# RG-LRU with a top-1 mixture of experts on one core: fixed slots at known rows, squares of eight blocks summed on TensorE, six weight halves cut by VectorE, narrow slots spread

## The chip, the cores and the metric

One core of a Trainium2 chip runs the whole program. The metric is the device time of one execution in microseconds (us), the median of the runs shown.

## The reference, cut to what matters

```
# recurrence, x, r_gate, i_gate: (4, 5056, 256)
log_a = 8 * sigmoid(r_gate) * log(clip(sigmoid(a_param)))
a_t   = exp(log_a)
xg    = sqrt(max(1 - a_t*a_t, 1e-6)) * sigmoid(i_gate) * x
h     = a_t[:, t] * h + xg[:, t]                 # for each t: y[:, t] = h
# mixture, y as x: (20224, 256), 8 experts, w1: (8, 256, 1024), w2: (8, 1024, 256)
logits = x @ w_gate;  e = argmax(logits)
out[token] = softmax(logits)[e] * sigmoid(x @ w_output_gate)[e] * (relu(x @ w1[e]) @ w2[e])
```

All inputs and the output are float32.

## The kernel before

**Products.** An fp32 operand is multiplied by a power of two and cut into an upper and a lower f16 half; each product is then three f16 matmuls. The power of two comes from a bound on the operand's norm.

**Tokens.** The 158 tiles of 128 tokens form 20 chunks of 8 tiles, a chunk being two blocks of 512 tokens (128 partitions x 1024 numbers). For a block, SP loads three tensors; ACT does tanh twice (L569, L572), exp (L579), a square (L583) and a root (L588); DVE does two products (L575, L591) and the scan (L622). The bound on the block's norm follows: in the first eight chunks ACT squares the block once more and sums (`top`, L661), in the later ones DVE takes a maximum; one matmul spreads the sum (L294) and DVE makes the scale (L299, L300). ACT then writes the upper half (L675), DVE the lower one (L680), and PE transposes and takes the logits (L701); ACT copies the transposed rows out (L708).

**Routing.** Of each chunk, DVE picks the expert of every token, PE counts ranks (L742, L744), and DVE adds the rank to the running end of each expert's region in `xs`, a buffer in DRAM (`positions`, `counts`). POOL then writes the rows there by 8 indirect transfers (`scatter_rows`, L389), one a tile.

**Weights.** The 16 weight units (w1 and w2 of 8 experts) go through load, a sum of squares by PE (`gram`, L475, bf16 matmuls of 128x128 blocks with themselves), an ACT square of the 128x128 result (L481), a total (L484), the scale (L488), an upper half (L508) and a lower half on DVE (L522). `MODES` names the engine of the upper half for each unit: S is ACT, D is DVE. `BOUNDS` names for each chunk the engine of the norm.

**Expert work.** A slot is a run of rows of one expert: transposing load from `xs` (L1060), w1 from DRAM (L1075), first product (`ph`, L1103), relu on ACT (L1118) and its lower half on DVE (L1121), second product (`po`, L1147), scaling by ACT (`ot`, L1160), indirect store by POOL (L1163). `po` has one buffer of two 128x256 parts; the first `po` matmul of a slot waits until ACT has read both parts of the slot ahead. Most slots are planned on the chip: 63 of 256 rows, 25 of 128 and 4 of 64 ran. Before them come eight fixed slots of 128 rows, one an expert, for the first chunk (`turn`, L902 to L1023). `round_plan` (L879) works out their first rows and limits by nine DVE operations, SP reads each first row into a register (L913), and DVE clips the row numbers so that a row that isn't the slot's own goes nowhere (L980). Because a fixed slot may read past the rows that its expert has so far, the second chunk's scatters wait for all eight loads:

```
past = fetched.get(c - 1, []) + ([tiles["fill"]] if c < NC and "fill" in tiles else [])
```

**Order.** All work is given to a planner (`in_order`) with an engine, a cost, a rank and what it follows; it plays the program through and writes each engine's instructions in that order. The tables `UNIT_RANK`, `CHUNK_RANK`, `UNIT_LOAD`, `SLACK`, `LAG`, `PACE` and others are the ranks and delays. Engines run their instructions strictly in the written order.

## Time and profile before

| | |
|---|---|
| runs | 1047.46, 1047.15, 1046.22 us; median 1047.15 |
| profiled execution | 1047.38 us, of which the span is 1045.7 |
| PE, ACT, DVE, POOL busy | 92%, 69%, 66%, 36% of the span |
| granted TensorE clock, mean | 0.965 |

The span runs from the first to the last instruction of the profile; the execution's own time is 1.68 us longer. A share of busy time is a mean over stages that have different limits, so the stretches further down tell more than this table.

### The profile page before, as it was taken

To read this page: it belongs to the slowest core of one execution; us is meant where nothing else is said; L and a number is where in the kernel's file an instruction comes from. 1 tells how busy PE (TensorE), PEld (TensorE's weight loads), DVE (VectorE), ACT (ScalarE), POOL (GpSimd) and SP (SyncE) were. 2 spreads that over 40 slices of the span, in tenths; PEclk is the share of its full clock that TensorE was granted. 3 is DMA by queue.
4 is the path that set the end of the run, shared out by engine and by line. 5 is a ranking of instruction groups with operands and counts; after the bars stand their busy time and mean duration, and the time that the engine had idled before them with its cause. 6 is when DMAs were issued, how large, how long until landed. Compare 5 with 4: busy or idle time off the path is not lost.

```text
span 1045.7 us, 29645 instructions
## 1 busy us (share of the span) xinstructions
PE 966.7 (92%) x9892; PEld 869.4 (83%) x9892; DVE 694.9 (66%) x1714; ACT 720.6 (69%) x1153; POOL 372.9 (36%) x346
## 2 busy tenths in 40 slices
PE   2567668999999999999999999999999999999997
PEld 2467667888889899999899998999999988899886
DVE  6788886688678686776867768586785763322212
ACT  7989989998986868668677676677767542332222
POOL 0040153543445343443525334262443434311211
PEclk9658889999999999999999999999999999999999
DMA  9995469999788888788778687778798566647683
GB/s 326 376 337 128 111 201 280 277 321 263 245 267 228 247 258 214 258 225 256 233 230 261 198 272 221 241 249 227 245 218 246 162 174 198 168 145 246 240 221 132
DMA packets 196528, 244.25 MB, mean 234 GB/s; under 512 B 119182, under 2 KB 130447, under 8 KB 196384
## 3 DMA queue, kind: packets, MB, share of 16 engines
q1 hardware_dynamic: 180656, 199.13, 64.7%
q0 software_dynamic: 15728, 43.17, 12.5%
q8 instruction: 94, 1.54, 0.6%
q14 instruction: 50, 0.41, 0.1%
HBM read 79.09 MB, written 45.97 MB: 120 GB/s over the span
## 4 chain that ended last, share of the span: by engine, by line
PE 70%; DMA 10%; issue 7%; ACT 5%; SPq 3%; POOL 3%; DVE 3%; POOLq 0%; DVEq 0%; ACTq 0%
PE po L1147 33%; PE ph L1103 33%; PE pt L701 3%; DMA w1r<-in_moe_w_dram 2%; POOL xs L389 2%; DMA ws<-w1r 2%; DMA xs<-rows_all,posi 1%; DMA xt<-in_x_dram 1%; DMA w2r<-in_moe_w_dram 1%; DMA rt<-in_r_gate_dram 1%; SPq L1060 1%; POOL out_dram L1163 1%; ACT w1r L508 1%; ACT rows_all L708 1%; DVE h L1121 1%
## 5 line engine op out<-in xcount | busy, mean ns | idle before, releaser
L1103 PE MATMUL ph<-xt,ws 128*128 128x256 f16 (+2 forms) x4416 | 487.5, 256 | 8.3 <-DMA ws<-w1r 3.0
L1147 PE MATMUL po<-w2r,h 128*128 (+1 forms) x3720 | 492.7, 272 | 2.3 <-ACT ot L1160 1.1
L1103 PEld LDWEIGHTS <-ws 128*128 128x128 f16 x4416 | 377.2, 99 | 48.5 <-issue 8.9
L1147 PEld LDWEIGHTS <-h 128*128 128x128 f16 (+1 forms) x3720 | 358.0, 98 | 46.0 <-issue 3.5
L1121 DVE SCALAR_TENSOR_TENSOR h<-ph,h 128x512 f16<-128x512 f32 (+1 forms) x310 | 208.2, 679 | 190.0 <-ACT h L1118 189.4
L1163 POOL DMA_INDIRECT out_dram<-ot,mt x155 | 171.5, 1107 | 394.2 <-ACT ot L1160 335.3
L1118 ACT ACTIVATE h<-ph 128x512 f16<-128x512 f32 (+1 forms) x310 | 181.1, 588 | 107.6 <-PE ph L1103 107.2
L389 POOL DMA_INDIRECT xs<-rows_all,posi x158 | 180.1, 1140 | 200.1 <-ACT h L1118 91.4
L1160 ACT ACTIVATE ot<-po,osc 128x256 f32<-128x256 f32 (+1 forms) x155 | 68.3, 471 | 145.1 <-PE po L1147 125.0
L708 ACT ACTIVATE rows_all<-pt 128x512 f16<-128x512 f32 x158 | 92.5, 597 | 11.0 <-PE pt L701 7.1
L622 DVE TENSOR_TENSOR_SCAN it<-rt,last,it 128x512 f32<-128x512 f32 (+4 forms) x78 | 96.1, 1241 | 0.7
L701 PE MATMUL pt<-iw,xt 128*128 128x160 f16 x632 | 72.7, 242 | 11.7 <-ACT xt L675 5.8
L712 DVE TENSOR_REDUCE lz<-pt 128x16 f32<-128x64 f32 x158 | 34.3, 221 | 63.2 <-PE pt L701 39.1
L701 PEld LDWEIGHTS <-xt 128*128 128x128 f16 x632 | 54.3, 102 | 16.7 <-ACT xt L675 6.3
L579 ACT ACTIVATE rt<-rt,lam 128x512 f32<-128x512 f32 (+1 forms) x80 | 61.1, 802 | 0.2
L680 DVE SCALAR_TENSOR_TENSOR xt<-it,sc,xt 128x1024 f16<-128x1024 f32 (+1 forms) x40 | 50.7, 1267 | 11.9 <-ACT xt L675 11.6
L575 DVE SCALAR_TENSOR_TENSOR xt<-it,xt 128x1024 f32<-128x1024 f32 (+1 forms) x40 | 48.3, 1207 | 9.7 <-DMA xt<-in_x_dram 6.6
L591 DVE SCALAR_TENSOR_TENSOR it<-it,xt 128x1024 f32<-128x1024 f32 (+1 forms) x40 | 48.3, 1208 | 8.6 <-ACT it L588 8.6
L675 ACT ACTIVATE xt<-it,sc 128x1024 f16<-128x1024 f32 (+1 forms) x40 | 45.2, 1129 | 4.3 <-DVE sc L300 4.2
L583 ACT ACTIVATE it<-rt 128x1024 f32<-128x1024 f32 (+1 forms) x40 | 41.9, 1047 | 5.9 <-DVE xt L575 4.3
L569 ACT ACTIVATE rt<-rt 128x1024 f32<-128x1024 f32 (+1 forms) x40 | 42.0, 1049 | 5.5 <-DMA rt<-in_r_gate_dram 5.3
L588 ACT ACTIVATE it<-it,quarter 128x1024 f32<-128x1024 f32 (+1 forms) x40 | 44.5, 1133 | 0.3
(159 smaller groups left out, 712.8 us busy)
## 6 DMA issues: line engine op xcount, KB each, us to landing
ws<-w1r SPq DMA_DIRECT2D x184, 512.0 KB
rt<-in_r_gate_dram SPq DMA_DIRECT2D x39, 512.0 KB
it<-in_i_gate_dram SPq DMA_DIRECT2D x39, 512.0 KB
xt<-in_x_dram SPq DMA_DIRECT2D x39, 512.0 KB
w1r<-in_moe_w_dram SPq DMA_DIRECT2D x7, 1024.0 KB
w2r<-in_moe_w_dram SPq DMA_DIRECT2D x7, 1024.0 KB
xs<-rows_all,posi POOLq DMA_INDIRECT x158
out_dram<-ot,mt POOLq DMA_INDIRECT x155
```

The costliest lines, as they stand in the source:

```text
L389: op = nc.gpsimd.indirect_dma_start(out=xs[:, :], out_offset=bass.IndirectOffsetOnAxis(ap=pos, axis=0), in_=rows.bitcast(F32), in_offset=None,
L579: nc.scalar.activation(r[:, h], r[:, h], AF.Exp, scale=lam[:, h:h + 1], bias=lam[:, h:h + 1])
L622: nc.vector.tensor_tensor_scan(H[:, h, lo:hi], A[:, h, lo:hi], H[:, h, lo:hi], first, op0=ALU.mult, op1=ALU.add)
L680: nc.vector.scalar_tensor_tensor(halves()[:, 1], H(), s_of(), halves()[:, 0], op0=ALU.mult, op1=ALU.subtract)
L701: nc.tensor.matmul(pt[:, k, h * P:h * P + PIECE], lhsT=halves()[:, k, h, (j % 4) * P:(j % 4 + 1) * P], rhs=iw[:, h, :], start=h == 0, stop ...
L708: nc.scalar.activation(rows_all[:, row_at[j], 0:META].rearrange("p (k h d) -> p k h d", k=2, h=ND), src, AF.Copy)
L1103: nc.tensor.matmul(ph[:, i], lhsT=ws[:, f // 2 % 2, a, c, f % 2 * P:(f % 2 + 1) * P], rhs=xt[:, b * ND + c, 0:w], start=k == 0, stop=k == ...
L1118: newest["relu"] = nc.scalar.activation(part(0, f0), tiles["ph", s, f0], AF.Relu).ins
L1121: nc.vector.scalar_tensor_tensor(part(1, f0), tiles["ph", s, f0], 0.0, part(0, f0), op0=ALU.max, op1=ALU.subtract)
L1147: nc.tensor.matmul(po[0:pw, j], lhsT=hh[:, a, f % 4, j * P:j * P + pw], rhs=w2r[:, bass.ds(eo + (b * NF + f) * D, D)], start=f + j + a + b ...
L1160: nc.scalar.activation(ot[0:pw], tiles["po", s][0:pw, j], AF.Copy, scale=tiles["osc", s][0:pw, j, :])
L1163: op = nc.gpsimd.indirect_dma_start(out=out[:, :], out_offset=bass.IndirectOffsetOnAxis(ap=tiles["mt", s][0:pw, j, 1:2].bitcast(I32), axis=0),
```

## The change

- The first 128 rows of each expert in the first chunk go to an area of their own behind the regions, 128 rows an expert at an address that is known beforehand. `round_plan`, the register loads and the clip are gone; `positions` of the first chunk has three more DVE operations and `counts` one more. Only the first chunk's scatters wait (for the filling with zeros); the second chunk's wait for no load.
- `BOUNDS` names P for the first four chunks. PE then multiplies the upper bf16 halves of the block's eight 128x128 parts with themselves into one 128x128 sum (`energy`, after.py L678), ACT squares that and sums it (`spread`, L684).
- `MODES` gives the upper halves of six w2 units to DVE (one operation of 128x2048 each, L511).
- The narrow slots are put in at every fourth place among the last wide ones and no longer all at one place.
- New ranks, loads and delays everywhere.

```diff
-REGION = 21760
+REGION = 20736
-MODES = 'SSSSSSSSSSSSSSSS'
+MODES = 'SDSDSDSDSDSDSSSS'
-BOUNDS = 'AAAAAAAADDDDDDDDDDDD'
+BOUNDS = 'PPPPAAAADDDDDDDDDDDD'
-LAG = 0.00102
+LAG = 0.00107
-SLACK = (0.324, 1.234, 2.066, 1.637, 1.622, 0.589)
-PACE = 9.7e-05
+SLACK = (0.187, 0.464, 1.348, 1.897, 0.524, 0.04)
+PACE = 8.94e-05
-THIN_AT = 6
+THIN_AT = 12
+THIN_GAP = 3
...
-        past = fetched.get(c - 1, []) + ([tiles["fill"]] if c < NC and "fill" in tiles else [])
+        past = [tiles["fill"]] if c < ROUNDS else []
...
+            def energy(key=key, H=H, m=m):
+                norm_tile(key)
+                upper = H().bitcast(BF16).rearrange("p h (t two) -> p h t two", two=2)
+                k = 0
+                for h in range(ND):
+                    for f in range(0, m, P):
+                        blk = upper[:, h, f:f + P, 1]
+                        nc.tensor.matmul(tiles["norm", key][:, P:2 * P], lhsT=blk, rhs=blk, start=k == 0, stop=k == ND * m // P - 1, skip_group_check=True)
+                        k += 1
+
+            def spread(key=key):
+                am = tiles["am", key] = small.tile([P, 1], F32, name=f"am_{key[0]}_{key[1]}", tag="am", bufs=4)
+                pn = tiles["norm", key]
+                nc.scalar.activation(pn[:, 2 * P:3 * P], pn[:, P:2 * P], AF.Square, accum_out=am)
...
+            if c < ROUNDS:
+                nc.vector.scalar_tensor_tensor(beyond, carry, -float(P + c * E * P), fixed, op0=ALU.add, op1=ALU.subtract)
+                nc.vector.scalar_tensor_tensor(pos, rank_in, float(P), wide(beyond), op0=ALU.is_ge, op1=ALU.mult)
+                nc.vector.scalar_tensor_tensor(pos, pos, float(c * E * P), wide(fixed), op0=ALU.add, op1=ALU.add)
+                nc.vector.tensor_tensor(pos, pos, rank_in, op=ALU.add)
...
-                nc.sync.dma_start_transpose(xt[:, :, 0:P], xs[bass.ds(row, P), 0:META // 2].bitcast(F16)),
+                nc.sync.dma_start_transpose(xt[:, :, 0:P], xs[first:first + P, 0:META // 2].bitcast(F16)),
...
-            nc.vector.tensor_scalar(ids_, ids_, tiles["turn_lim", c][:, e:e + 1], float(N), op0=ALU.max, op1=ALU.min)
```

**ACT, around the last weight unit's square (L481 before, L482 after; `pg` is a unit's sum of squares, `w2r` an upper half of w2, `xt` a block's upper half, `am` a norm sum).** Before:

```order
69 L661 ACTIVATE xt_0_394,am_0_776<-it_0_322 128x1024
70 L481 ACTIVATE pg_754,sq_780<-pg_754 128x128
71 L508 ACTIVATE w2r<-w2r,wsc 128x2048
72 L675 ACTIVATE xt_0_394<-it_0_322,sc_806 128x1024
73 L481 ACTIVATE pg_782,sq_822<-pg_782 128x128
74 L569 ACT_TABLE_LOAD
75 L569 ACTIVATE rt_0_774<-rt_0_774 128x1024
76 L708 ACTIVATE rows_all<-pt_0_838 128x512
77 L708 ACTIVATE rows_all<-pt_1_844 128x512
78 L661 ACTIVATE xt_4_544,am_4_871<-it_4_459 128x1024
```

With the change:

```order
67 L482 ACTIVATE pg_732,sq_756<-pg_732 128x128
68 L684 ACTIVATE norm_0_764,am_0_792<-norm_0_764 128x128
69 L482 ACTIVATE pg_774,sq_799<-pg_774 128x128
70 L694 ACTIVATE xt_0_400<-it_0_328,sc_802 128x1024
71 L482 ACTIVATE pg_810,sq_829<-pg_810 128x128
72 L569 ACT_TABLE_LOAD
73 L569 ACTIVATE rt_0_753<-rt_0_753 128x1024
74 L732 ACTIVATE rows_all<-pt_0_838 128x512
75 L732 ACTIVATE rows_all<-pt_1_844 128x512
76 L579 ACTIVATE rt_0_753<-rt_0_753,lam 128x512 x2
```

The last weight square is row 73 before and row 71 now. Ahead of it stand three of the eight block squares and six `w2r` halves of 128x2048 before, and three small squares (L684) and no such half now, but eight table loads instead of six. Behind it stand five block squares and one such half before, five small squares and one half now.

**POOL, from the first chunk's scatters on (`xs` scatters, `out_dram` stores of the fixed slots).** Before:

```order
20 L389 DMA xs<-rows_all,posi_612 174080x264 x8
21 L1014 DMA out_dram<-ot_t_0_1082,mt_t_0_813 20224x256
22 L1014 DMA out_dram<-ot_t_1_1254,mt_t_1_831 20224x256
23 L1014 DMA out_dram<-ot_t_2_1462,mt_t_2_854 20224x256
24 L389 DMA xs<-rows_all,posi_1331 174080x264 x8
25 L1014 DMA out_dram<-ot_t_3_1588,mt_t_3_953 20224x256
```

With the change:

```order
20 L390 DMA xs<-rows_all,posi_658 168192x264 x8
21 L1018 DMA out_dram<-ot_t_0_1126,mt_t_0_852 20224x256
22 L390 DMA xs<-rows_all,posi_1194 168192x264 x4
23 L1018 DMA out_dram<-ot_t_1_1291,mt_t_1_868 20224x256
24 L390 DMA xs<-rows_all,posi_1194 168192x264 x3
25 L1018 DMA out_dram<-ot_t_2_1404,mt_t_2_885 20224x256
26 L390 DMA xs<-rows_all,posi_1194 168192x264
27 L1018 DMA out_dram<-ot_t_3_1566,mt_t_3_975 20224x256
```

The second chunk's eight scatters stood behind the stores of fixed slots 0, 1 and 2; now the last of them alone stands behind that of slot 2.

**PE, at the border of two wide slots in the middle of the program (`po` the second product, `ph` the first; one row for each group of six matmuls of a kind, or for their first).** Before:

```order
9973 L1147 MATMUL po_7727<-w2r,h_1_7644 128x256
...
10008 L1103 MATMUL ph_6_7864<-xt_33_7372,ws_1_7609 128x256
...
10020 L1103 MATMUL ph_0_7902<-xt_34_7674,ws_0_7714 128x256
...
10046 L1147 MATMUL po_7945<-w2r,h_0_7751 128x256
```

With the change:

```order
9294 L1151 MATMUL po_7221<-w2r,h_1_7172 128x256
...
9329 L1107 MATMUL ph_6_7323<-xt_30_6874,ws_1_7103 128x256
...
9341 L1107 MATMUL ph_0_7361<-xt_31_7038,ws_0_7218 128x256
...
9355 L1151 MATMUL po_7376<-w2r,h_0_7278 128x256
```

Between the last `po` of a slot and the first of the next stood 18 `ph` matmuls (6 of `ph_6`, 12 of `ph_0`); now 12 stand there (6 and 6). So it is at 33 of the borders of the 63 wide slots that run; at most others, transposes (L701, now L725) stand between as well, before and now, and six `ph` matmuls fewer.

## Rows read from the trace of the kernel before

**Rows 1.** Stretches of 25 and 100 us: busy us and instructions, PE clock, DMA share, GB/s

```profile
core 0: us, PE busy (x) PEld busy (x) DVE busy (x) ACT busy (x) POOL busy (x), PEclk, DMA share, GB/s
25.00:50.00 25.00, 12.83 (x122) 11.69 (x122) 18.07 (x30) 23.10 (x33) 0.00 (x0) 0.66 1.06 376
50.00:75.00 25.00, 16.42 (x143) 15.22 (x143) 22.27 (x61) 22.57 (x39) 12.76 (x8) 0.58 1.06 379
75.00:100.00 25.00, 17.57 (x192) 16.18 (x193) 21.45 (x42) 22.54 (x30) 1.47 (x1) 0.77 0.52 104
100.00:125.00 25.00, 17.91 (x214) 15.64 (x212) 23.07 (x56) 24.88 (x36) 2.21 (x2) 0.82 0.35 100
125.00:150.00 25.00, 18.21 (x205) 15.83 (x204) 19.30 (x54) 22.84 (x35) 12.72 (x12) 0.93 0.69 212
150.00:175.00 25.00, 19.31 (x220) 18.44 (x221) 17.81 (x37) 23.88 (x33) 12.52 (x11) 0.80 0.91 258
225.00:250.00 25.00, 25.00 (x272) 22.77 (x271) 18.67 (x41) 24.59 (x41) 11.42 (x10) 1.00 0.89 296
400.00:500.00 100.00, 100.00 (x972) 90.36 (x970) 71.53 (x179) 71.81 (x119) 38.47 (x34) 1.00 0.85 241
```

**Rows 2.** ACT's groups by form, 0 to 260 us: busy, mean ns, idle before

```profile
L508 ACT ACTIVATE w2r<-w2r,wsc 128x2048 f16<-128x2048 f32 x7 | 13.9, 1990 | 0.9 <-DVE w2r L522 0.9
L661 ACT ACTIVATE xt<-it 128x1024 f32<-128x1024 f32 x13 | 13.7, 1052 | 2.8 <-DVE it L622 2.8
L661 ACT ACTIVATION_READ_ACCUMULATOR xt<-it 128x1 f32 x13 | 2.5, 192 | 0.0
L481 ACT ACTIVATE pg<-pg 128x128 f32<-128x128 f32 x16 | 4.1, 258 | 4.9 <-PE pg L475 4.9
L481 ACT ACTIVATION_READ_ACCUMULATOR pg<-pg 128x1 f32 x16 | 3.0, 185 | 0.0
L588 ACT ACT_TABLE_LOAD x11 | 14.1, 1283 | 0.2
```

**Rows 3.** PE in order of time, the last weight unit's sum of squares

```profile
75.30 1.03 PE L475 MATMUL pg<-fw 128*128 128x128 bf16 x8 [0.67 <-DMA fw<-in_moe_w_dram]
```

**Rows 4.** ACT in order of time, up to the last weight unit's square

```profile
77.16 1.15 ACT L675 ACTIVATE xt<-it,sc 128x1024 f16<-128x1024 f32 x1 [0.53 <-DVE sc L300]
78.21 0.26 ACT L481 ACTIVATE pg<-pg 128x128 f32<-128x128 f32 x1
```

**Rows 5.** DVE's groups by form, 0 to 260 us

```profile
L522 DVE SCALAR_TENSOR_TENSOR w2r<-w2r,wsc 128x2048 f16<-128x2048 f32 x7 | 16.4, 2348 | 0.0
L522 DVE SCALAR_TENSOR_TENSOR w1r<-w1r,wsc 128x1024 f16<-128x1024 f32 x14 | 17.7, 1278 | 0.6 <-ACT w1r L508 0.6
L980 DVE TENSOR_SCALAR mt_t<-mt_t,turn_lim 128x1 int32<-128x1 int32 x8 | 1.6, 203 | 0.0
```

**Rows 6.** POOL in order of time: first scatter of the first two chunks

```profile
58.26 1.36 POOL L389 DMA_INDIRECT xs<-rows_all,posi  x1 [50.01 <-DVE carry L786]
...
128.85 1.07 POOL L389 DMA_INDIRECT xs<-rows_all,posi  x1 [2.53 <-DVE lz L712]
```

**Rows 7.** SP's queue: loads of fixed slots 0 and 7, load of planned slot 0

```profile
77.44 1.32 SPq L920 DMA_TRANSPOSE xt_t<-xs  x1
...
122.51 1.22 SPq L920 DMA_TRANSPOSE xt_t<-xs  x1
...
146.65 1.25 SPq L1060 DMA_TRANSPOSE xt<-xs  x1
```

**Rows 8.** PE in order of time at a border of two wide slots

```profile
500.42 2.13 PE L1103 MATMUL ph<-xt,ws 128*128 128x256 f16 x18
502.38 1.36 PE L1147 MATMUL po<-w2r,h 128*128 x11
```

**Rows 9.** ACT in order of time at the same border

```profile
500.67 0.84 ACT L1160 ACTIVATE ot<-po,osc 128x256 f32<-128x256 f32 x2 [1.92 <-issue]
501.40 0.60 ACT L1118 ACTIVATE h<-ph 128x512 f16<-128x512 f32 x1
501.88 1.07 ACT L583 ACTIVATE it<-rt 128x1024 f32<-128x1024 f32 x1
```

**Rows 10.** PE's waits from 250 to 1000 us: total, times, longest

```profile
PE po L1147 <- ACT ot L1160: 0.9, 1, 0.9
```

**Rows 11.** PE in order of time in the second narrow slot

```profile
994.41 0.35 PE L1103 MATMUL ph<-xt,ws 128*128 128x64 f16 x6 [0.39 <-DMA ws<-w1r]
```

More of the change, by code (lines that the diff above doesn't have):

```diff
@@ L31 @@
 RAW = 0
-TURNS = (840, 880, 920, 920, 940, 940, 940, 940)
+TURNS = (860,)
 RESERVE = {128:800,256:1500}
@@ L376, in tables @@
         nc.vector.tensor_scalar(carry, iota_e, float(REGION), None, op0=ALU.mult)
-        nc.vector.tensor_scalar(base, iota_e, float(REGION), None, op0=ALU.mult)
+        nc.vector.tensor_scalar(fixed, iota_e, float(P), float(E * REGION), op0=ALU.mult, op1=ALU.add)
         nc.vector.memset(zrow, 0.0)
@@ L397, in scatter_rows @@
                 ins, k.name, mybir.DependencyInfo(mybir.DependencyClass.Sync, mybir.DependencyReason.DATA),
-                reason="rows come over the filling, and behind the slots of fixed place that read past the rows of an expert",
+                reason="rows come over the filling",
             )
@@ L785, in counts @@
             pk = tiles["pk", c]
-            nc.vector.tensor_tensor(carry, carry, pk[:, nt * E:(nt + 1) * E], op=ALU.add)
+            held = pk[:, nt * E:(nt + 1) * E]
+            if c < ROUNDS:
+                nc.vector.tensor_scalar(beyond, held, -float(P), 0.0, op0=ALU.add, op1=ALU.max)
+                held = beyond
+            nc.vector.tensor_tensor(carry, carry, held, op=ALU.add)
         quick = rank + QUICK
@@ L796, in chunk @@
         wt = work("DVE", 0.85, weights, [zs] + copied, quick, uses=rused)
-        ps = work("DVE", 0.85, positions, [pk, chain["carry"]], quick, uses=[pu])
-        ct = work("DVE", 0.14, counts, [ps, chain["carry"]] + ([chain["plan"]] if chain["plan"] else []), quick, uses=[pu])
+        ps = work("DVE", 0.85 + (0.55 if c < ROUNDS else 0.0), positions, [pk, chain["carry"]], quick, uses=[pu])
+        ct = work("DVE", 0.14 + (0.15 if c < ROUNDS else 0.0), counts, [ps, chain["carry"]] + ([chain["plan"]] if chain["plan"] else []), quick, uses=[pu])
         chain["carry"] = ct
@@ L877, in plans @@
                 plan(group[k:k + GROUP])
[L879 to L900 removed]
     def turn(c, e):
         rank = ROUND_RANK[c] + e * TURN + 0.0001
[L905 removed]
+        first = E * REGION + (c * E + e) * P
         s = ("turn", c, e)
@@ L912, in fetch @@
         def fetch():
-            _, (row,) = nc.values_load_multi_w_load_instructions(
-                tiles["turn_row", c][0:1, e:e + 1], engines=(SP,), min_val=0, max_val=E * REGION - P,
-                skip_runtime_bounds_check_because="rows are counted on the chip",
-            )
             xt = tiles["xt16", s] = xtp.tile([P, 4, SLOT], F16, name=f"xt16_t{c}_{e}", tag="xt16")
@@ L925, in fetch @@
             after_scatters(loads, c)
-            fetched.setdefault(c, []).extend(op.ins for op in loads)
-        rows = [v for cc in range(c + 1) for v in routed[cc]]
-        fw = work("SP", 2.0, fetch, [ready, xold, mold] + rows, rank, dma=1.15, uses=[xu, mu, vuse])
-        fetches.setdefault(c, []).append(fw)
+        fw = work("SP", 1.3, fetch, [xold, mold] + routed[c], rank, dma=1.15, uses=[xu, mu])
         hus = [rings["hh"].new() for _ in range(2)]
@@ L1053, in fetch @@
             _, (row,) = nc.values_load_multi_w_load_instructions(
-                tiles["plan", s][0:1, 0:1], engines=(SP,), min_val=0, max_val=E * REGION - w,
+                tiles["plan", s][0:1, 0:1], engines=(SP,), min_val=0, max_val=last_row - w,
                 skip_runtime_bounds_check_because="rows are counted on the chip",
@@ L1223, in rglru_moe @@
     chunk(0)
-    if ROUNDS:
-        round_plan(0)
     scaled = []
@@ L1245, in rglru_moe @@
             chunk(c)
-            if c < ROUNDS:
-                round_plan(c)
         plans(c)
@@ L1254, in rglru_moe @@
         k = len(wide) - SPARE - THIN_AT
-        for s in wide[:k] + thin[:E - THIN_SPARE] + wide[k:] + thin[E - THIN_SPARE:] if thin else wide:
+        order = list(wide)
+        for i, s in enumerate(thin[:E - THIN_SPARE]):
+            order.insert(k + i * (THIN_GAP + 1), s)
+        for s in order + thin[E - THIN_SPARE:]:
             if s in spare and s < n_wide and not late:
```

105 lines of the change are left out of this document (47 added, 58 removed).

## Prediction

> **What bounds the kernel now.** I read the stretches first, because the page's means (PE 92%) mix stages with different limits. From 225 us on PE has no gap, and a stretch of the middle shows PE busy 100.00 of 100 us while ACT and DVE have a quarter free [rows 1]. There only fewer or cheaper matmuls would help, and the change removes none. So the time is PE's fixed work plus what PE loses ahead of 225 us, plus a tail. From 25 to 175 us PE is busy 12.8 to 19.3 of 25 us, at granted clocks of 0.58 to 0.93. ACT is busy 22.5 to 24.9 of 25 in the same stretches: it is the bound. DVE, at 21.5 and 23.1 of 25 between 75 and 125 us, is close behind. Up to 75 us the DMA engines are also full (shares 1.06 and 1.06).
>
> Second, ACT's groups by form give prices: 1.990 us for an upper half of w2, 1.052 + 0.192 = 1.244 for a block's square with its accumulator, 0.258 + 0.185 = 0.443 for a unit's 128x128 square, 1.283 for a table load [rows 2]. Third, PE's and ACT's rows in order of time show the last weight unit: its sum of squares waited 0.67 us for its load and ran from 75.30 to 76.33 [rows 3]; ACT took its square at 78.21, behind an upper half of a block that ended then [rows 4].
>
> **The sum, against the profiled execution of 1047.38 us (0.23 above the median, which I neglect).**
>
> *ACT.* Eight squares at 1.244 become eight like the units' 128x128 square at 0.443: 8 x 0.801 = 6.4 us less. Six halves less are 6 x 1.990 = 11.9. Two more table loads are 2.6 more. Together 15.7 us less on the engine that bounds. But ACT works in its written order, and the last weight's square is a meeting point. The order shows three squares, all six halves and both table loads ahead of it: 2.4 + 11.9 - 2.6 = 11.7 us. The load comes no sooner, as the DMA engines are full and the bytes of weights are the same, so I take this part to become a wait for DMA. What is kept of it is at most the 1.9 us from 76.33 to 78.21; I take 1.5. Behind it stand five squares: 5 x 0.801 = 4.0 us, at ACT busy 90% or more until PE is full, so all of it counts. **ACT: -5.5**, with 0 (another engine takes over) and -15.7 (the planner moved enough chunk work ahead that none of it waits) as ends.
>
> *PE.* Each of eight blocks gets eight 128x128 bf16 matmuls. A unit's eight take 1.03 us [rows 3], so 8.2 us in all, 5.2 of it behind the meeting point. There PE has 6 to 7 idle us in each 25 [rows 1], which hides them, unless one stands ahead of work that ACT waits for. Between 0 and +5.2 I take **+1.0**.
>
> *DVE.* It gets six 128x2048 `tensor_scalar` operations, which no row shows. The nearest row, its lower half of the same shape, takes 2.348, and a half as long one 1.278 [rows 5]; so 7.7 to 14.1 us more; I take 2.348, the same columns. By the order one stands just ahead of the last weight's scale and two behind it: 7.0. Eight clips at 0.203 [rows 5] and nine operations of `round_plan` of like size leave: 17 x 0.2 = 3.4 less; four operations in `positions` and `counts` add 0.8. Net +4.4 behind the meeting point, against 5.5 us idle between 75 and 125 us [rows 1]. It just fits; I take **+0.5**, with 0 and +4.4 as ends. Ahead of it 7.0 us more must fit into 25 to 75 us, where DVE had 9.7 idle.
>
> The Trainium skill, page "VectorE: DVE Perf Modes", section "The perf-mode tier table", gives an fp32 `tensor_scalar` of 2048 columns 1.227 us, half its two-tensor price. By that the six would be 7.4 us and this term 0; the sum would be 0.5 us lower. No row here shows it.
>
> *Fixed slots.* The first chunk's scatters began at 58.26 [rows 6], fixed slot 0 was loaded at 77.44 and slot 7 at 122.51 [rows 7]. The second chunk's scatters waited for that last load and began at 128.85 [rows 6]; planned slot 0 was loaded at 146.65 [rows 7]. Now only POOL's order holds them: the eighth stands behind the store of fixed slot 2. I expect planned slot 0's load some 10 us earlier. That is worth something only while PE has gaps and ACT has time for the relu, and ACT has none (23.9 of 25 from 150 us on). Between 0 and -5.7 (PE's idle of 150 to 175 us), I take **-1.0**, near the lower end because ACT decides.
>
> *Narrow slots.* They have one wait for weights in the rows, 0.39 us [rows 11]. Spread among wide ones they lose it: **-0.4**, between -0.8 and +0.5.
>
> *Borders of wide slots.* `po` has one buffer, so PE must be covered while ACT reads it. PE left the last `po` at 500.42, ACT had read both parts at 501.51, 1.09 us later [rows 9], and 18 `ph` matmuls covered 1.96 us, until 502.38 [rows 8]. In all of 250 to 1000 us this wait cost 0.9 us, once [rows 10]. Now 12 matmuls stand there, 1.96 x 12/18 = 1.31 us of cover: 0.22 us remain. If ACT is free at the border that is enough; I take **0**, with +13 (below) as the upper end.
>
> Sum: -5.5 + 1.0 + 0.5 - 1.0 - 0.4 = **-5.4, so 1042.0 us**.
>
> **The rivals.**
>
> *The covers are too short (slower).* At the border a block's square of 1.07 us comes a relu behind the reads [rows 9]; had it stood ahead of them, they would end up to 1.07 later and PE would stand 1.07 - 0.22 = 0.85 us. ACT is 72% busy in the middle [rows 1], about half of it in such long operations. If a quarter of the 62 borders are hit with 0.85, it costs 62/4 x 0.85 = 13 us: 1055. It outweighs the gain from 7.5/62 = 0.12 us a border on. For it: all borders lost six matmuls of cover, and a loss here is on the saturated engine, so nothing gives it back. Against it: at 29 of the 62 borders transposes still stand in between, and the order puts the second products there by a plan that knows ACT's work.
>
> *DVE or the first chunk takes over (no change).* DVE's net 4.4 us do not fit, since its operations also wait, and the first chunk's scatters start 4 us later, behind one more table load and more DVE work, with the fixed slots behind them. That eats all: about 1047.
>
> *The freed ACT time carries (larger gain).* If chunk work fills ACT's 11.7 us ahead of the last weight, about 7 of it would be kept besides: 1035. For it: the planner reordered everything. Against it: three block squares stand ahead of that point in both orders.
>
> *POOL is held up.* POOL writes the first chunk's scatters from 58.26 on [rows 6] while DVE's new operations run. If one kept POOL from its work as long as it lasts, two of 2.348 would make the fixed slots later by up to 4.7, of which about half is seen: 1042.0 + 2.3 = 1044.3. The Trainium skill, page "SBUF — State Buffer", section "Who interferes with whom", says that a DVE `tensor_scalar` in a two-port mode locks GpSimd out of shared ports for the whole instruction. No row of this kernel shows such a lock, and by the order most of the six don't stand beside the scatters.
>
> **How the numbers follow.** A measurement of this kernel can tell about 0.2%, 2.1 us, from no change. The forecast has 0.45 (its own range 1038 to 1046; 0.03 of it within 2.1 us of before), the larger gain 0.13, POOL held up 0.05, no change 0.19 (0.13 within, 0.06 slower), short covers 0.18. Faster: 0.42 + 0.13 + 0.05 = 0.60; same: 0.03 + 0.13 = 0.16; slower: 0.06 + 0.18 = 0.24. The range runs from 1033, under the larger gain, to 1054, which leaves out the worse half of the short covers.
>
> **What would show it.** Right: PE full from about 220 us on, ACT with gaps for DMA ahead of the last unit's square, at about 77; DVE over 22 of 25 between 75 and 125 us; the second chunk's scatters begun before 120. The covers show as a wait of `po` for ACT's `ot` from 250 us on, 0.9 us before: over 7 us would make me wrong. A last weight square well before 75 would mean the larger gain; scatters of the first chunk past 63 and PE full only at 225 the case of no change. A new price for the 128x2048 `tensor_scalar` corrects the DVE term.

## The result and the profile after

The changed kernel took 1052.13 us (median of 5, 1051.24 to 1055.96) where the kernel before took 1046.22 on the same chip: ratio 1.0051, 95% interval [1.0036, 1.0067]. It is slower by half a per cent; 1042.0 and a gain were forecast. On another chip the pair came out at 1.0036 [1.0021, 1.0052] (e12_again below).

Chips differ, for both kernels alike: before takes 1047 us on some (here called chips of the first kind) and 1061 to 1067 on others (the second kind), so every ratio below is taken on one chip.

The profile of the first result caught that run's slowest execution (1055.96, span 1054.3). I read the new kernel mostly from e12_again, the same kernel on a chip of the first kind, whose span of 1048.6 lies 2.9 over that of before (3.3 between the medians on its chip). Stretches of e12_again, columns as in [rows 1]:

```profile
core 0 of [0], span 1048.6 us
core 0: us, PE busy (x) PEld busy (x) DVE busy (x) ACT busy (x) POOL busy (x), PEclk, DMA share, GB/s
25.00:50.00 25.00, 14.27 (x131) 12.80 (x130) 20.79 (x36) 20.39 (x32) 0.00 (x0) 0.86 1.06 377
50.00:75.00 25.00, 18.26 (x155) 16.90 (x155) 21.95 (x60) 19.24 (x38) 8.26 (x8) 0.57 1.06 377
75.00:100.00 25.00, 18.15 (x199) 16.76 (x197) 24.11 (x36) 21.53 (x31) 0.99 (x1) 0.74 0.54 131
100.00:125.00 25.00, 14.08 (x151) 12.06 (x151) 22.10 (x55) 22.61 (x34) 8.48 (x8) 0.73 0.44 139
125.00:150.00 25.00, 20.07 (x267) 17.98 (x267) 22.70 (x59) 24.39 (x38) 7.72 (x7) 1.00 0.42 112
150.00:175.00 25.00, 19.94 (x243) 17.44 (x244) 18.95 (x34) 22.53 (x35) 10.67 (x10) 0.93 1.02 295
...
225.00:250.00 25.00, 21.26 (x205) 18.10 (x204) 17.72 (x37) 23.00 (x37) 11.14 (x11) 1.00 0.88 267
```

ACT did get its gaps: 20.39, 19.24 and 21.53 of 25 us up to 100, against 23.10, 22.57 and 22.54 [rows 1]. DVE rose to 24.11 between 75 and 100. The decisive row is the last: PE, which had no idle between 225 and 250 us before [rows 1], now loses 3.74 us there. And from 250 us to the end PE is busy for 786.76 us before and for 790.44 in e12_again: at 250 it has 3.7 us more work left. PE's waits of e12_again from 200 to 300 us (total, times, longest) say on what:

```profile
PE ph L1107 <- DMA xt<-xs: 2.4, 1, 2.4
PE ph L1107 <- DMA ws<-w1r: 2.1, 1, 2.1
PE po L1151 <- ACT h L1122: 1.0, 2, 0.7
```

The first wait is for the rows of a slot: the first slot that needs the fifth chunk's scatters. Its load in SP's queue, before and in e12_again, each in order of time:

```profile
242.44 1.30 SPq L1060 DMA_TRANSPOSE xt<-xs  x1
```

```profile
244.16 1.27 SPq L1064 DMA_TRANSPOSE xt<-xs  x1
```

In e12_again PE has nothing else to do when it gets there; before, other work lasted until it got there, and it shows no wait. PE in order of time, the first product of that slot, before and in e12_again:

```profile
245.86 3.44 PE L1103 MATMUL ph<-xt,ws 128*128 128x256 f16 x30
```

```profile
248.99 3.44 PE L1107 MATMUL ph<-xt,ws 128*128 128x256 f16 x30 [2.43 <-DMA xt<-xs]
```

I call the start of this load **the date**: the end moves with it. In every profile on chips of the first kind the rest of the span after it is nearly the same, 803 to 807 us, while the date moves by 14. (The last columns are worked out. A chunk's ranks are PE's `pk`: the second row `pk<-oh,before` in time for the second chunk, the fifth for the fifth.)

```
kernel (profile)                  pk, chunk 2   pk, chunk 5    date    date - pk 5    span   span - date
before                               106.09       217.44      242.44      25.0      1045.7      803.3
e9_before                            105.81       216.29      241.38      25.1      1044.7      803.3
e10 before, halves on DVE            108.62       219.71      244.84      25.1      1048.9      804.1
e12 changed                          105.91       216.24      244.16      27.9      1048.6      804.4
e13 changed, 18 matmuls at borders   106.86       219.29      249.18      29.9      1053.8      804.6
e11 changed, slots' steps moved      111.17       218.47      246.41      27.9      1052.6      806.2
changed, first result                106.20       219.24      248.32      29.1      1054.3      806.0
e15 changed, halves on ACT           111.63       222.98      251.93      29.0      1058.0      806.1
e14 changed, both parts undone       114.26       226.12      255.09      29.0      1062.1      807.0
```

One trace is not a median: e12, e13 and the first result have the same order up to the slots ahead of the date, and their dates still lie 5 us apart (the last two are the slowest executions of their runs). So a date tells little below some 5 us, and the 3.7 us by which the last column varies are as large as the loss. The size of the loss comes from the medians; the traces tell where it arises.

So the first question is why freeing ACT did not make the chunks earlier. **ACT's gain arrives at the second chunk's logits and is lost in DVE's order right there.** Up to that chunk's `pk`, ACT's groups by form add up to 102.0 us before and 91.9 in e12_again: 10.1 less. Without the table loads it would be 91.8 against 76.5, 15.3 less, but the new order has 12 loads of 1.283 us up to there where the old one has 8. And `pk` comes at 105.91 against 106.09, no earlier. DVE in order of time, before (L723 is the last step that needs ACT's part, L736 what `pk` waits for):

```profile
102.45 0.22 DVE L723 TENSOR_SCALAR un<-sc,gun 128x8 int32<-128x8 int32 x1
102.58 2.58 DVE L522 SCALAR_TENSOR_TENSOR w1r<-w1r,wsc 128x1024 f16<-128x1024 f32 x2
105.08 0.22 DVE L732 SCALAR_TENSOR_TENSOR eq<-df,rev 128x64 f32<-128x64 f32 x1
105.34 0.22 DVE L735 TENSOR_REDUCE mx<-eq 128x8 f32<-128x64 f32 x1
105.59 0.22 DVE L736 TENSOR_TENSOR oh<-eq,mx 128x64 f16<-128x64 f32 x1
```

and in e12_again (the same two steps are L747 and L760):

```profile
97.44 0.23 DVE L747 TENSOR_SCALAR un<-sc,gun 128x8 int32<-128x8 int32 x1
97.58 1.22 DVE L591 SCALAR_TENSOR_TENSOR it<-it,xt 128x1024 f32<-128x1024 f32 x1
98.83 2.46 DVE L622 TENSOR_TENSOR_SCAN it<-rt,last,it 128x512 f32<-128x512 f32 x2
101.32 0.17 DVE L625 COPY last<-it 128x2 f32<-128x2 f32 x1
101.41 1.22 DVE L575 SCALAR_TENSOR_TENSOR xt<-it,xt 128x1024 f32<-128x1024 f32 x1
102.56 0.27 DVE L984 TENSOR_SCALAR osc_t<-mt_t,undo 128x1 f32<-128x1 f32 x1
102.74 2.47 DVE L523 SCALAR_TENSOR_TENSOR w2r<-fw,wsc,w2r 128x1024 f16<-128x1024 f32 x2
105.13 0.22 DVE L756 SCALAR_TENSOR_TENSOR eq<-df,rev 128x64 f32<-128x64 f32 x1
...
105.63 0.22 DVE L760 TENSOR_TENSOR oh<-eq,mx 128x64 f16<-128x64 f32 x1
```

`un` is 5.0 us earlier, about the 5.5 that were forecast for ACT. But between `un` and `oh` lie 8.19 us now and 3.14 before: the third chunk's gates and the last cut of a w2 unit have been put there. PE sees nothing of the gain; it stands for that `oh` (PE in order of time, e12_again):

```profile
96.94 1.50 PE L951 MATMUL ph_t<-xt_t,w1r 128*128 128x128 f16 x24
105.91 0.23 PE L766 MATMUL pk<-oh,before 128*128 128x64 f16 x1 [7.47 <-DVE oh L760]
106.27 1.01 PE L678 MATMUL norm<-it 128*128 128x128 bf16 x8
111.01 0.59 PE L295 MATMUL norm<-am,ones 128*128 128x1 f32 x2 [3.73 <-ACT norm L684]
```

So at this chunk nothing is gained. (The `pk` of this one chunk does not decide the end alone: see e11 below.) **What is lost on top lies further on, between the fifth chunk's ranks and the date:** 25.0 to 25.1 us in the three traces in the old order, 27.9 to 29.9 in the six in the new one. Before, PE's ranks of that chunk and then the first and the last of its eight scatters on POOL:

```profile
217.44 0.19 PE L742 MATMUL pk<-oh,before 128*128 128x64 f16 x1
```

```profile
220.91 0.97 POOL L389 DMA_INDIRECT xs<-rows_all,posi  x1 [0.30 <-issue]
...
236.41 1.15 POOL L389 DMA_INDIRECT xs<-rows_all,posi  x1 [0.30 <-issue]
```

and in e12_again:

```profile
216.24 0.19 PE L766 MATMUL pk<-oh,before 128*128 128x64 f16 x1
```

```profile
221.13 0.96 POOL L390 DMA_INDIRECT xs<-rows_all,posi  x1 [2.32 <-issue]
...
238.28 1.91 POOL L390 DMA_INDIRECT xs<-rows_all,posi  x1 [0.30 <-issue]
```

In e12_again the ranks are 1.2 us earlier than before and the date is 1.7 later. Of these 2.9 us, 1.4 lie between the ranks and the first scatter and 1.7 between the first and the last, among which POOL has three stores of slots instead of two. This is read from the traces; no run here moves these steps by themselves.

The new operations themselves are short. DVE's and ACT's groups by form from 0 to 260 us and PE's groups of the whole span, e12_again:

```profile
L511 DVE TENSOR_SCALAR w2r<-w2r,wsc 128x2048 f16<-128x2048 f32 x6 | 7.7, 1282 | 0.1
```

```profile
L684 ACT ACTIVATE norm<-norm 128x128 f32<-128x128 f32 x8 | 2.1, 264 | 2.2 <-PE norm L678 2.0
L684 ACT ACTIVATION_READ_ACCUMULATOR norm<-norm 128x1 f32 x8 | 1.5, 193 | 0.0
```

```profile
L678 PE MATMUL norm<-it 128*128 128x128 bf16 x64 | 7.1, 276 | 0.0
```

### The profile page after: what moved, and what is told of

Its sections match the earlier page's. It is cut to its first block, busy times and chain, and to the rows that moved or that the text cites. A ratio compares the mean times of both kernels' runs of the same rounds, so it can differ in the third digit from the quotient of the medians.

```text
span 1054.3 us, 29719 instructions
## 1 busy us (share of the span) xinstructions
PE 973.7 (92%) x9956; PEld 873.4 (83%) x9956; DVE 698.0 (66%) x1707; ACT 711.2 (67%) x1149; POOL 366.1 (35%) x346
## 4 chain that ended last, share of the span: by engine, by line
PE 73%; DMA 9%; ACT 8%; issue 4%; DVE 3%; SPq 1%; POOL 1%; POOLq 0%; ACTq 0%; DVEq 0%
PE po L1151 34%; PE ph L1107 33%; PE pt L725 3%; DMA ws<-w1r 2%; DMA xt<-in_x_dram 2%; DMA w1r<-in_moe_w_dram 2%; ACT rows_all L732 1%; DMA w2r<-in_moe_w_dram 1%; ACT rt L579 1%; PE ph_t L951 1%; PE po_t L1001 1%; POOL out_dram L1167 1%; DVE xt L575 1%; DVE xt L699 1%; ACT it L588 1%
## 5 line engine op out<-in xcount | busy, mean ns | idle before, releaser
L1151 PE MATMUL po<-w2r,h 128*128 (+1 forms) x3720 | 505.1, 272 | 5.3 <-ACT h L1122 1.6
L1107 PE MATMUL ph<-xt,ws 128*128 128x256 f16 (+2 forms) x4416 | 499.1, 255 | 10.5 <-DMA ws<-w1r 8.5
L1167 POOL DMA_INDIRECT out_dram<-ot,mt x155 | 166.6, 1075 | 343.4 <-ACT ot L1164 279.5
L725 PE MATMUL pt<-iw,xt 128*128 128x160 f16 x632 | 71.5, 240 | 10.3 <-DVE xt L699 3.4
L736 DVE TENSOR_REDUCE lz<-pt 128x16 f32<-128x64 f32 x158 | 34.0, 222 | 55.5 <-ACT rows_all L732 26.6
L725 PEld LDWEIGHTS <-xt 128*128 128x128 f16 x632 | 53.2, 101 | 16.1 <-issue 6.0
L572 ACT ACTIVATE it<-it 128x1024 f32<-128x1024 f32 (+1 forms) x40 | 42.2, 1055 | 3.7 <-DMA it<-in_i_gate_dram 3.6
```

Source lines behind the costliest of these rows:

```text
L725: nc.tensor.matmul(pt[:, k, h * P:h * P + PIECE], lhsT=halves()[:, k, h, (j % 4) * P:(j % 4 + 1) * P], rhs=iw[:, h, :], start=h == 0, stop ...
L1107: nc.tensor.matmul(ph[:, i], lhsT=ws[:, f // 2 % 2, a, c, f % 2 * P:(f % 2 + 1) * P], rhs=xt[:, b * ND + c, 0:w], start=k == 0, stop=k == ...
L1151: nc.tensor.matmul(po[0:pw, j], lhsT=hh[:, a, f % 4, j * P:j * P + pw], rhs=w2r[:, bass.ds(eo + (b * NF + f) * D, D)], start=f + j + a + b ...
L1167: op = nc.gpsimd.indirect_dma_start(out=out[:, :], out_offset=bass.IndirectOffsetOnAxis(ap=tiles["mt", s][0:pw, j, 1:2].bitcast(I32), axis=0),
```

## The experiments

Theories at the start: (O) the new order costs, the parts save; (W) one piece of it, the late last w1 halves, holds the slots' weights; (B) the shorter covers at the borders cost; (A) ACT's time ahead of the last weight's square is worth nothing. (The letters in the quoted expectations are those of each text by itself.) Ranks set the whole order, so most kernels below leave the order alone and change one thing in place.

**1. On a chip of the second kind (before 1061.27).** e1_again is the changed kernel unchanged.

> The changed kernel once more, as the yardstick of this batch. Every theory: the median within 1050 to 1054 us. The profile taken before was of an execution of 1055.96 us, 4 us over the median; if the 23 us by which the first weights of planned slots were loaded later (158.04 us against 135.10) are a property of the order and not of that one execution, they stand here again at 155 to 161 us, and PE again waits 6 us or more for slot weights ahead of 260 us.

Measured 1074.11, 1.0112 [1.0081, 1.0144]: the loss is more than twice as large on this kind of chip. The expected times were for the other kind. The named signs did not come either: the first weights are loaded at 167.17, and PE waits 2.5 us for slot weights ahead of 260 us. (On a chip of the first kind they are loaded at 157.42, in e12_again.)

e2_w1_early gives three w1 units an earlier rank:

```diff
-UNIT_RANK = (..., 2125.187, ..., 2071.655, 94.077, 1911.079, 778.463)
+UNIT_RANK = (..., 700.0, ..., 700.0, 94.077, 700.0, 778.463)
```

> The changed kernel with the ranks of the last three w1 units alone set from 2125, 2072 and 1911 to 700, so that their halves are cut earlier and the slots' first weight loads, which need all w1 halves, stand ahead of the slots' row loads in SP's order. Theory A (late w1 halves keep the planned slots off PE until 163 us): the first slot weights are loaded at 130 to 145 us, the first product of planned slot 0 begins by 153, and the time falls by 4 to 8 us, to 1044 to 1048. Theory B (the new norm by PE holds up PE's queue, or the missing cover of the wide slots costs): the time stays within 2 us of 1052.

e3_old_ranks has the changed structure with all ranks, loads and delays of before, e4_new_ranks the reverse.

```diff
-UNIT_RANK = (-32.393, -264.014, -294.491, 2128.445, ...)
+UNIT_RANK = (-418.188, 1238.039, 483.025, 96.75, ...)
```

> The changed kernel's structure (own rows of the fixed slots, norm by PE for eight blocks, six upper halves by DVE, narrow slots spread) with all ranks, loads, slacks and paces of the kernel before. Theory A (the new ranks cost, the structure saves): 1038 to 1045 us. Theory B (the structure costs): 1050 us or more.

> The kernel before with the new ranks, loads, slacks and paces and nothing else. Theory A (the new ranks cost 5 to 15 us by themselves): 1052 to 1062 us. Theory B (the structure costs and the ranks are good): at or under 1046 us.

Measured: e2 1101.32, 1.0369 [1.0334, 1.0405]; e3 1077.39, 1.0144 [1.0105, 1.0182]; e4 1098.09, 1.0345 [1.0307, 1.0382]. Each lets the planner write the whole order anew. None comes near a gain: e2 and e4 are slower than the changed kernel (1.0112), e3 is not told apart from it (intervals overlap). So both readings of e2 failed, and e3 and e4 tell only that orders written from other ranks lie 1.4 to 3.7% over before; they do not separate (O) from (W). From here on I moved works by hand.

**2. On another chip of the second kind (before 1060.72),** with e5_again as yardstick.

> The changed kernel once more as the yardstick of its batch: 0.3 to 1.4% over the kernel before.

Measured 1073.35, 1.0117 [1.0095, 1.0139].

e6_w1_moved moves only the late w1 cuts forward, and three weight loads of slots ahead of the first planned rows in SP's queue:

```diff
+    early = [at[v] for v in (("hi", 12, 1), ("lo", 12, 1), ("hi", 14, 0), ("lo", 14, 0), ("hi", 14, 1), ("lo", 14, 1))]
+    loads = [at["ws", 0, 0], at["ws", 0, 1], at["ws", 1, 0]]
...
+    k = order.index(at["lo", 12, 0]) + 1
+    order[k:k] = early
+    k = max(order.index(at["xs", 0]), k + len(early))
+    order[k:k] = loads
```

> The changed kernel in the very same order but for nine works: the last three w1 halves (ACT and DVE) stand directly behind the first half of the unit ahead, and the three first weight loads of planned slots stand directly ahead of the first row load of a planned slot in SP's queue; nothing else moves. Theory A (the late w1 halves keep planned slots off PE): first slot weights at 130 to 140 us, first planned product 5 to 10 us sooner, 3 to 8 us less than the changed kernel in the same batch. Theory B (ACT and DVE have no time for them earlier, what they push back costs as much): within 2 us of it.

Measured 1080.07, 1.0190 [1.0173, 1.0207]: 6.7 us worse than e5, where a gain or no change was expected. (W) falls: the late weights (157.42 in e12_again, 135.10 before) are not what costs, and cutting them earlier takes time from the chunks. In e6 the third chunk's `pk` comes at 158.92, in e5 at 150.42.

e7_cover puts 18 matmuls between the `po` of two blocks again, in PE's order alone:

```diff
+    for w in [w for w in order if w.tag and w.tag[0] == "po" and w.tag[2] == 0 and w.tag[3] == 256]:
...
+        if v.tag[0] == "ph":
+            order.insert(n + 1, w)
+            order.pop(k)
```

> The changed kernel in the same order, but at each border of two 256-row slots the first group of second products is put behind the next group of first products, so that 18 matmuls stand between the last second product of a slot and the first of the next, as before the change. Theory C (the cover of 12 is too short where ACT is called late): 3 us or more less than the changed kernel on a chip where the border shows a gap of 0.3 us or more, and nothing (within 2 us) on a chip where it shows none. Theory A: within 2 us on either.

Measured 1068.82, 1.0083 [1.0066, 1.0100]: 4.5 us better than e5; the intervals overlap slightly. So on this chip the longer cover probably pays, but not in the way (B) says. A border in e5, PE and then ACT in order of time:

```profile
518.61 1.47 PE L1107 MATMUL ph<-xt,ws 128*128 128x256 f16 x12
520.25 0.92 PE L1151 MATMUL po<-w2r,h 128*128 x6 [0.17 <-ACT ot L1164]
```

```profile
519.36 0.84 ACT L1164 ACTIVATE ot<-po,osc 128x256 f32<-128x256 f32 x2 [2.51 <-PE po L1151]
```

The 12 matmuls do not quite cover ACT's two reads, but by 0.17 us only, under the 0.3 that the expectation named. From 260 us on all waits of `po` for ACT's `ot` are 0.8 us in e5 and 0.6 in e7, so the 4.5 are not there. Where they come from is open.

e8_undone keeps the changed order and undoes both parts in place: ACT scales the six halves and squares the four chunks' blocks, the 64 matmuls are gone.

```diff
-                by_scale(hi_by, d[:, 0], fw)
+                by_scale("ACT", d[:, 0], fw)
...
-                nc.scalar.activation(pn[:, 2 * P:3 * P], pn[:, P:2 * P], AF.Square, accum_out=am)
+                nc.scalar.activation(tiles["xt", key][:, :, 0:m], H(), AF.Square, accum_out=am)
```

> The changed kernel in the same order, with the two parts that take work off ACT undone in place: ACT itself cuts the six w2 halves and squares the four chunks' blocks over 128x1024, each at the place in the order where the new operation stood; the 64 matmuls are gone. ACT does 15.8 us more ahead of 175 us. Theory A (ACT's freed time only became waits): within 3 us of the changed kernel. Theory D (ACT is still the bound and the freed time counts): 5 us or more over the changed kernel.

Measured 1080.28, 1.0192 [1.0176, 1.0208]: 6.9 us worse than e5, as theory D has it. The parts do save, in this order.

**3. On a chip of the first kind (before 1047.74).** e9_before is the kernel before, for its profile.

> The kernel before itself, for a profile from the chips on which it takes 1061 us and not 1047. Every theory: within 0.5% of the kernel before. If the 14 us more come from the same places as the changed kernel's, PE loses some of them ahead of 250 us and some at the transposes that wait for DVE's lower halves from 300 to 860 us, and none at the borders of the wide slots, where 18 matmuls stand.

Measured 1047.5, 1.0003 [0.9991, 1.0015]. The chip was of the first kind, so the question about the slower chips got no answer: no profile of the kernel before from the second kind exists here.

e10_before_modes takes the order of before and gives the six halves to DVE in place:

```diff
-                by_scale(hi_by, d[:, 0], fw)
+                by_scale("DVE" if u in (1, 3, 5, 7, 9, 11) else hi_by, d[:, 0], fw)
```

> The kernel before in its own order, with one part of the change put in place: DVE cuts the upper halves of the same six w2 units (six operations of 1.28 us in place of six of 1.99 us on ACT). Theory D (ACT is the bound and freed time counts): 3 to 8 us less than before. Theory A (freed time ahead of the last weight's square only becomes a wait, as forecast): within 2 us of before.

Measured 1049.6, 1.0016 [1.0005, 1.0027]. 11.9 us taken from ACT gain nothing in the old order; it is even 1.9 slower, and `pk` of the second chunk comes 2.5 later than in before (108.62). That fits (A) as to the time, but the trace shows ACT waiting for DVE and not for the weights' load. ACT in order of time, e10, ahead of the last weight's square, which came at 78.21 before [rows 4] and now comes at 82.31:

```profile
81.26 1.15 ACT L675 ACTIVATE xt<-it,sc 128x1024 f16<-128x1024 f32 x1 [5.12 <-DVE wsc L488]
82.31 0.26 ACT L481 ACTIVATE pg<-pg 128x128 f32<-128x128 f32 x1
```

e11_turn1 moves fixed slots' steps in the changed kernel, so that PE has work in the hole at 98 us:

```diff
+    group = [at[v] for v in (("ht", 1, 0), ("hl", 1, 0), ("ht", 1, 4), ("hl", 1, 4), ("ht", 2, 0), ("hl", 2, 0))]
+    group += [at["pt", 1, f] for f in range(8)]
...
+    k = order.index(at["pk", 1])
+    order[k:k] = group[6:]
...
+    order[k:k] = group[:6]
```

> The changed kernel in the same order but for 14 works around 98 us: ACT's three relus of fixed slots 1 and 2 and DVE's lower halves of them stand ahead of the last w2 unit's cut, and PE's second products of fixed slot 1 stand ahead of the ranks of the second chunk, for which PE waited 7.5 us with the clock falling behind. Theory E (the new order of the first 130 us leaves PE idle where work was there, and that is lost for good): 4 to 9 us less than the changed kernel (ratio to before of 1.003 to 1.008 where the changed kernel has 1.0115). Theory A (ACT's total up to 250 us decides, PE's idle here is made up): within 2 us of it.

Measured 1054.76, 1.0068 [1.0051, 1.0085], against 1.0051 [1.0036, 1.0067] and 1.0036 [1.0021, 1.0052] of the changed kernel on such chips: no gain, so theory E fails. PE's wait for `oh` shrank from 7.5 to 4.1 us, a new one of 2.9 for ACT came ahead of it, and `pk` of the second chunk came 5 us later (111.17). The date is still inside what the changed kernel shows by itself (246.41; 244.16 and 248.32), so a late `pk` of this one chunk is made up again here.

**4. Parts and order apart, on a chip of the first kind (before 1047.25).** All four on one chip.

> The changed kernel once more, the yardstick of this group. 1.005 of before if the chip is one of the faster kind (before near 1047), 1.011 if before is near 1061.

> Eighteen matmuls again between the po of a block and the next, nothing else moved. If the borders cost something only where ACT starts its read of the last po late (the slower chips), this is the changed kernel within 1 us on a chip with before near 1047, and 4 to 5 us under it on a chip with before near 1061. If the cover pays everywhere, 4 to 5 us under it on either.

> The new order with the old parts: ACT scales the six halves and squares the four chunks' blocks, the 64 matmuls are gone. If the order is the loss and the parts give back, this is 6 to 8 us over the changed kernel and 11 to 13 over before (1.011 of before on a fast chip). If the parts are worth nothing, it is the changed kernel within 2 us.

e15_halves_undone is e8's first edit alone.

> Of the two parts only the halves are undone, in place: ACT scales all six again (6 x 1.99 = 11.9 us more on ACT, 6 x 1.28 = 7.7 us less on DVE). If only what lies behind the last weight's square counts (the reading of the prediction), the halves are worth little and this is 0 to 2 us over the changed kernel, while the squares carry the 6 to 8 of the fully undone one. If any ACT time of the first 175 us counts, the halves carry two thirds: 4 to 5 us over.

Measured:

```
before                                          1047.25
e12_again          1.0036 [1.0021, 1.0052]      1050.54
e13_cover          1.0051 [1.0033, 1.0069]      1053.54
e15_halves_undone  1.0090 [1.0071, 1.0110]      1057.20
e14_all_undone     1.0133 [1.0110, 1.0156]      1062.32
```

This settles (O). With the old halves and squares the new order is 15.1 us slower than before (the new rows of the fixed slots and the spread narrow slots are in it too); the two parts give back 11.8 of it, the halves 6.7 (1057.20 less 1050.54), the squares 5.1. The direction was expected, the sizes were not: 6 to 8 for both and at most 5 for the halves. On the chip of e8 the same two parts gave back 6.9. And (B) costs nothing here: with the long cover the kernel is no better (3.0 us over e12, where 1 was expected; intervals overlap), and PE's waits of e12_again from 260 us on hold only this row for it (total, times, longest):

```profile
PE po L1151 <- ACT ot L1164: 0.6, 2, 0.4
```

The trace of e14 shows the order's cost at the same place of DVE as above:

```profile
105.79 0.23 DVE L738 TENSOR_SCALAR un<-sc,gun 128x8 int32<-128x8 int32 x1
...
113.98 0.22 DVE L751 TENSOR_TENSOR oh<-eq,mx 128x64 f16<-128x64 f32 x1
```

`oh` is at 105.59 before, 113.98 here and 105.63 in e12_again. Of the order's 8.4 us, 3.3 lie ahead of `un` and 5.0 between `un` and `oh`; the parts bring `un` forward by 8.35 (105.79 to 97.44), which just makes up for it. Further on in e14 against before, 8.7 us stand at the fifth chunk's ranks, 12.7 at the date and 16.4 at the end of the span.

**5. Can the swallowed time be had back?** On a chip of the second kind (before 1065.62). e16_chunk1_first takes the second chunk's small steps out of the way:

```diff
+    names = ("cn", "pk", "ps", "ct", "sm", "zs", "wt")
+    own = [at[n, 1] for n in names]
...
+    k = order.index(at["ch", 1])
+    order[k + 1:k + 1] = own[:2]
+    k = behind(k + 2, "DVE", 1)
+    order[k:k] = own[2:4]
...
```

> The second chunk's small steps go first, nothing else moves: DVE takes eq, mx, oh right behind un and the positions one operation later, ahead of the third chunk's gate scans; PE takes pk there; ACT takes the second exponential of that chunk 9 instructions earlier. If DVE's order at this place swallowed the gain, pk of that chunk comes at about 99 instead of 106, its scatters begin some 7 us earlier (107 instead of 114.5), and the end is 3 to 5 us earlier: 0 to 2 us under before. If the chunks behind (the third chunk's gates, now later on DVE by 2 to 3 us) or PE's own order hold the end, pk and the scatters come earlier all the same and the end is the changed kernel's within 1.5 us, or later by the 2 to 3.

> The changed kernel, the yardstick of this pair: 1.003 to 1.005 of before on a chip with before near 1047, 1.011 on one with before near 1061.

Measured: e17 1076.58, 1.0098 [1.0070, 1.0125]; e16 1071.83, 1.0058 [1.0033, 1.0083]. That is 4.75 us less, within the 3 to 5 that were expected though far from "under before", and the intervals overlap a little. The traces bear it out: `pk` at 101.84 (108.23 in e17), the date at 253.39 (257.23). PE in order of time, e16, shows the wait that came in its place:

```profile
101.84 0.20 PE L799 MATMUL pk<-oh,before 128*128 128x64 f16 x1 [0.59 <-DVE oh L793]
...
116.34 0.59 PE L324 MATMUL norm<-am,ones 128*128 128x1 f32 x2 [9.68 <-ACT norm L715]
```

e18_chunk1_slots, on a further chip of the second kind (before 1067.38), adds the steps behind that wait to e16's moves: ACT's square goes right behind the exponential, the fixed slots' steps of e11 forward, fixed slot 1's second products ahead of the wait.

```diff
+    k = max(order.index(at["ex", 1]), order.index(at["en", 2, 0])) + 1
+    order[k:k] = [square]
+    k = order.index(gates)
+    order[k:k] = twos
```

> As e16_chunk1_first, and besides: ACT takes the small square of the third chunk's first block right behind the exponential of the second chunk, 10 instructions earlier, and the relus of fixed slots 1 and 2 ahead of the last w2 cut; DVE their lower halves there; PE the 24 second products of fixed slot 1 ahead of the wait for that square. If the order of these few steps was what the new order cost, PE's idle of 106 to 116 (9.7 us in e16) falls under 3 us, the rows of the fifth chunk's first slot are loaded 4 to 6 us earlier than in the changed kernel without the moves, and the time is 0.993 to 1.000 of before on a chip with before near 1047, 1.000 to 1.005 on one near 1061. If PE only trades that wait for another (as when the same relus were moved alone), it is 0.999 to 1.003 or 1.005 to 1.009, as e16.

Measured 1077.95, 1.0120 [1.0089, 1.0151], six runs from 1071.88 to 1085.15. A miss on both readings: PE's wait only shrank from 9.7 to 7.5 us, and the time is that of the changed kernel, though `pk` of the second chunk is earlier still (100.73; the trace is of the fastest of the six). So e16's gain stands as likely, not as settled, and no version here beats the kernel before. The remaining part of the order's 15 us (its 8.4 at the second chunk taken off) is not pinned to single works; some 4 of it arise between the fifth chunk's ranks and the date (29.0 us in e14, 25.0 before). The narrow slots and the first chunk's new rows were not tried by themselves, since taking them out makes the planner write another order.

## Why the prediction was wrong

**The step that failed.** The sum has a term for each operation that goes or comes and none for the new order, which was put at nothing without a reason; and it counts ACT's freed time in full "until PE is full". The runs show the reverse weights: the new order costs 15.1 us and the two parts give back 11.8. What ACT gains at the second chunk is used up by DVE's work between `un` and `oh`, 8.19 us instead of 3.14.

**The bound** was read rightly in the main: ACT with DVE close behind sets how early the chunks come, and PE then runs almost without gaps. But I took PE to be full from 225 us on whatever happened. Before, it still had work when the fifth chunk's rows came (the date, 242.44); a date 1.7 us later opened a gap of 2.4. And "no gap" from 225 on was too strong even for before: from 250 to 275 us PE is busy for 23.95 of 25.

**ACT, -5.5: right where it was worked out, then lost.** The last weight's square came at 76.26 instead of 78.21 [rows 4], 1.95 kept where I took 1.5. The small squares took 0.264 + 0.193 where I took 0.443. I counted two more table loads; up to the second chunk's `pk` there are four, 5.1 us. `un` of the second chunk came 5.0 earlier. What failed here is "at ACT busy 90% or more until PE is full, so all of it counts": from `un` on it was not ACT that the chunk waited for. Nor is the time ahead of the last weight's square worth nothing: in the new order the halves, of which I kept at most the 1.5 of that stretch, give back 6.7.

**DVE, +0.5: the price was high, the place was wrong.** I summed the operations that the change adds (and over-priced them: 1.282 us instead of 2.348, 7.7 in all instead of 14.1, so that the time fits DVE better than I held). What counted was not in the list of added operations: the new order puts 5.0 us more of DVE's old work between `un` and `oh`. The Trainium skill, page "VectorE: DVE Perf Modes", section "The perf-mode tier table", had the price nearly right (1.227), and by it the term would have been 0, with the sum still wrong in sign.

**What no term held: the rest of the order.** I costed the added and removed operations and took the order otherwise as neutral, though the diff gave new ranks everywhere. With the two other parts it costs 15.1 us on a chip of the first kind (e14_all_undone). The parts, which I put at -5.5 + 1.0 + 0.5 = -4.0, are worth -11.8 in it and, for the halves, nothing in the old one (e10_before_modes): they have no price apart from an order. That the measured time is only 10 us off is in part luck: a cost of 15.1 that was not in the sum and a gain three times as large as the -4.0 in it nearly cancel.

**PE grams, +1.0:** 7.1 us of matmuls, and still the squares with them are worth -5.1 (e14 against e15). So PE's idle time probably hid most of them; no run has them alone.

**Fixed slots, -1.0:** planned slot 0's rows were loaded at 141.85 instead of 146.65 [rows 7], 4.8 earlier and not 10, though the second chunk's scatters began at 114.38 instead of 128.85 [rows 6]; their weights came 22 later. What the new rows are worth by themselves no run shows; moving the weights forward cost more (e6).

**Narrow slots, -0.4:** no wait for `ws` is left from 260 us on in e12_again, so this held as far as the trace tells it.

**Borders, 0 with +13 above:** right on the chips where the forecast was to be met (e13); on one of the second kind 4.5 (e7), inside the bounds. The sign that I named for the short covers, over 7 us of `po` waiting for `ot`, came on neither kind: 0.6 in e12_again, 0.8 in e5_again.

**The other rivals.** "DVE or the first chunk takes over" came nearest: `pk` of the second chunk is unchanged to 0.2 us, and the first chunk's scatters began at 63.98 against 58.26 [rows 6], past the 63 named as its sign. It was DVE, but through the place of its old work and not through the added operations, and I let it end at no change. "POOL is held up" was not put to the test: in e12_again none of DVE's six new operations runs beside the first chunk's scatters (45.48 and 74.74 are the nearest starts, the scatters lie between 63.98 and 74.4), so its condition is not met, and no run here shows whether the lock of which the Trainium skill, page "SBUF — State Buffer", section "Who interferes with whom", speaks would matter.

## What to carry to other kernels

When a change comes with a new order, costing the operations that it adds and removes prices only half of it: follow one item of the pipeline (here the second chunk, from logits to `oh` to ranks) through both orders on every engine and count what stands between its steps. Time freed on the bounding engine is worth what the next in-order queue behind it leaves over. And look for the last date that the saturated engine depends on: here span minus that date was 803 to 807 us in nine traces, so a gain ahead of it that does not move it did little for the end. Follow the item all the way to that date: in e12_again the fifth chunk was ahead of before at its ranks and behind at its load.

## What was not expected of the hardware

The same program takes 1047 us on some chips and 1061 to 1067 on others, and the changed kernel 1050 to 1052 and 1073 to 1077: a change can cost 0.4% on one and 1.1% on another. Of the 23.6 us between the spans of e5_again and e12_again, the same kernel, the larger part arises early: the second chunk's ranks come 2.4 us later (108.31), the third's 10.0 (150.42 against 140.41), and from 250 us on PE is still busy for 804.3 us instead of 790.4. After the date the two kinds differ too (803 to 807 us to the end of the span, 812 to 819 in eight traces from the second kind). A part of that is a wait: from 260 to 900 us PE waited for DVE's `xt` 4.9 us in e5_again,

```profile
PE pt L725 <- DVE xt L699: 4.9, 8, 1.7
```

and 0.5 in e12_again from 260 us to the end. What makes the chips differ, no run here shows.
